# Retention and two feed-forward networks on one core: weight words converted through a parametric ReLU, the hidden layer carried in turns

## The chip, the cores and the metric

The kernel runs on one core of a Trainium2 chip. Its engines work side by side, each through its own queue in order: TensorE (PE; its weight loads are PEld), VectorE (DVE), ScalarE (ACT), GpSimd (POOL) and SyncE (SP), which issues nearly all DMAs. The metric is the device time of one execution in microseconds.

## What is computed

Three steps follow each other: a masked, decaying attention without softmax, and two feed-forward networks over all 2304 tokens. The weights come as float64 and are split in the kernel into two fp32r parts each.

```python
scores = q @ k^T / sqrt(64)                       # 4 batches, 8 heads, 576 tokens, 64 wide
x = (scores * where(i >= j, gamma[h] ** (i - j), 0)) @ v
x = x as (2304, 512)
h = x @ w_in                                      # 512 -> 2048
y = (h * cos(h)) @ w_out                          # 2048 -> 512
h = y @ w2_in
g = where(h >= 1, h, where(h <= -1, 0, (h + 1) ** 2 / 4))
out = g @ w2_out
```

## The kernel before

The tokens of the first network are cut in five blocks (`BLOCKS`: 256 and four times 512), its hidden layer in 16 chunks of 128. A slot is one chunk of one block: `mm1` makes h in 12 matmuls (three products of high and low parts, four slices each), `actA`, `actB` and `actC` make h cos h out of it, `mm2`, two slots later, adds its share of the output in 12 more. Blocks 0 and 1 run interleaved while the weights are still being converted, one chunk of `w_in` (wi) and one of `w_out` (wo) for each pair of slots; a converted wi is also stored (wd) for blocks 2 to 4. The attention of a block's tokens runs before the block (blocks 0 and 1) or between the slots of the block ahead of it. The second network follows in 168 steps of a product scheme with seven products for eight (`product`, `after_product`, `piece`, `group`); its weights are converted in the background of blocks 2 to 4 (`spill_wi2`, `spill_wo2`).

The order on each engine is made by a scheduler, which works from the order of the program, the dependencies, the buffers of the pools and its own estimate of durations. So an operation that falls away can change the order elsewhere.

A weight chunk arrives as 128 x 512 words of 64 bit, seen as two 32-bit halves (raw; the low half is word 0, the high half word 1). Chunks of the first network from number 4 on are loaded twice, the second time shifted by a half word into rsh, so that one shift (L150) makes the low mantissa bits. `begin` (L134) reads the high half as an fp32 and scales it by 2^-112 on ScalarE into X. `signed` (L141 to L143) shifts X to an fp32 exponent and mantissa, takes the sign bit from the high half again and merges it into W, and cuts W to its power of two in X. L158, on ScalarE, rounds W to the high part; L159, on VectorE, makes the low part from C and X. The tag raw has two buffers, X, W and C two each; the next load into a raw buffer waits for the last reader of its high half, which for twice-loaded chunks is L142.

The first network's h stands in PSUM (blocks 0 and 1 copy it to SBUF first, L431). `actA` finds the whole turns by adding and subtracting MAGIC = 1.5 * 2^23 on ScalarE (L433, L434) and subtracts them from h on VectorE (L435); `actB` takes Sin and Square (L440, L441); `actC` multiplies by h (L455) and splits the result in gh (L447, ScalarE) and gl (L448, mostly GpSimd). TensorE's mm2 (L400 to L402) needs both. `copy_out` brings a finished block to SBUF with a factor.

Of the kernel before, what the change touches and what calls it, by code (L numbers as in the profile page):

```python
# [13 lines left out]
AF = mybir.ActivationFunctionType  # L14
ALU = mybir.AluOpType
# [20 lines left out]
LEAD = 3  # L36
TWICE = 4
MAGIC = 1.5 * 2.0 ** 23
INV2PI = 0.15915494309189535
TWOPI = 6.2831854820251465  # L40
SQRT2 = 1.4142135623730951
GAMMA = [1.0 - 2.0 ** (-5 - h) for h in range(H)]
# [23 lines left out]
def retention_moe_kernel(ctx: ExitStack, tc: tile.TileContext, qk, kv, win1, wout1, win2, wout2, mask, vtab, ptab, out):  # L66
    nc = tc.nc
    V, A, G, SY, PE = nc.vector, nc.scalar, nc.gpsimd, nc.sync, nc.tensor
# [25 lines left out]
    def behind(later, earlier):  # L94
        tc.add_manual_dep(later.ins, earlier.ins.name, mybir.DependencyInfo(mybir.DependencyClass.NoSync, mybir.DependencyReason.SCHED_ONLY), reason="pace")
# [31 lines left out]
    def begin(L, i, c, after=None, late=False):  # L127
        raw, raw2 = raws.pop((L, i, c))
        hi = raw[:, :, 1].bitcast(F32)
        if late:  # L130
            X, W = [wp.tile([P, DM], F32, tag=f"wo{k}", name="XW"[k - 1]) for k in (1, 2)]
        else:
            X, W = [cv.tile([P, DM], F32, tag=k, name=k) for k in "XW"]
        i0 = A.activation(X, hi, AF.Copy, scale=2.0 ** -112)  # L134
        if after is not None:
            behind(i0, after)
        return raw, raw2, X, W, late

    def signed(hi, X, W, odd):
        Xi, Wi = X.bitcast(I32), W.bitcast(I32)  # L140
        V.tensor_scalar(out=Xi, in0=Xi, scalar1=3, scalar2=odd, op0=ALU.logical_shift_left, op1=ALU.bitwise_or)  # L141
        V.scalar_tensor_tensor(out=Wi, in0=hi, scalar=-0x80000000, in1=Xi, op0=ALU.bitwise_and, op1=ALU.bitwise_or)  # L142
        V.tensor_scalar(out=Xi, in0=Wi, scalar1=-0x800000, scalar2=None, op0=ALU.bitwise_and)  # L143

    def convert(begun, o, after=None):
        raw, raw2, X, W, late = begun
        lo, hi = raw[:, :, 0], raw[:, :, 1]
        C = wp.tile([P, DM], I32, tag="wo3", name="C") if late else cv.tile([P, DM], I32, tag="C", name="C")
        if raw2 is not None:
            i0 = V.tensor_scalar(out=C, in0=raw2.bitcast(I32)[:, 1:1 + 2 * DM:2], scalar1=7, scalar2=None, op0=ALU.logical_shift_left)  # L150
        else:
            i0 = V.tensor_scalar(out=C, in0=hi, scalar1=23, scalar2=None, op0=ALU.logical_shift_left)
        if after is not None:
            behind(i0, after)
        if raw2 is None:
            V.scalar_tensor_tensor(out=C, in0=lo, scalar=9, in1=C, op0=ALU.logical_shift_right, op1=ALU.bitwise_or)
        signed(hi, X, W, 1)
        A.activation(o[:, 0, :], W, AF.Copy)  # L158
        return V.scalar_tensor_tensor(out=o[:, 1, :], in0=C, scalar=2.0 ** -43, in1=X, op0=ALU.mult, op1=ALU.mult)  # L159

# [2 lines left out]
    def make_wi1(c, begun, after=None):  # L163
        t = wr.tile([P, 2, DM], F32R, tag="wi", name="wi")
        convert(begun, t, after)
        SY.dma_start(out=wd[0, 0, c], in_=f(t))
        wi[0, c] = t

    def make_wo1(c, begun, after=None):
        t = wp.tile([P, 2, DM], F32R, tag=f"wo{c}", name=f"wo{c}")  # L170
        convert(begun, t, after)
        wo[0, c] = t

    def spill_wo2(c, begun):
        t = wp.tile([P, 2, DM], F32R, tag="wo5", name="cw") if begun[-1] else wr.tile([P, 2, DM], F32R, tag="wi", name="cw")
        done.append(convert(begun, t))
        SY.dma_start(out=wd[1, 1, c], in_=f(t))
# [4 lines left out]

    def to_fp32(begun, v):
        raw, _, X, W, _ = begun
        signed(raw[:, :, 1], X, W, 0)
        V.scalar_tensor_tensor(out=X, in0=raw[:, :, 0].bitcast(U32), scalar=2.0 ** -52, in1=X, op0=ALU.mult, op1=ALU.mult)
        done.append(V.tensor_tensor(out=v, in0=W, in1=X, op=ALU.add))

# [215 lines left out]
    def copy_out(e, t, y, scale):  # L404
        if e % 2 == 0:
            A.activation(t, y, AF.Copy, scale=scale)
        else:
            V.tensor_scalar(out=t, in0=y, scalar1=scale, scalar2=None, op0=ALU.mult)

    def evac(s):  # L410
        l, c = slots[s]
        if c != NC - 1:
            return
        o, n = BLOCKS[l]
        per = 512 // n
        for e, y in enumerate(yb.pop(l)):
            t = stp.tile([P, 512], F32, tag="st", name="st")
            copy_out(e, t, y, -1.0)
            SY.dma_start(out=yd[:, e * per:(e + 1) * per, o:o + n], in_=t.rearrange("p (k n) -> p k n", k=per))

    mark = [None]

    def actA(s):
        l, c = slots[s]
        n = BLOCKS[l][1]
        h = hp[s][:, :n]
        t = act.tile([P, 512], F32, tag="t", name="t", bufs=3)[:, :n]
        if l < 2:

            hp[s] = xp.tile([P, 512], F32, tag="x", name="hs")  # L430
            A.activation(hp[s][:, :n], h, AF.Copy)  # L431
            h = hp[s][:, :n]
        mark[0] = A.activation(t, h, AF.Copy, scale=INV2PI, bias=MAGIC)  # L433
        A.activation(t, t, AF.Copy, bias=-MAGIC)  # L434
        V.scalar_tensor_tensor(out=t, in0=t, scalar=-TWOPI, in1=h, op0=ALU.mult, op1=ALU.add)  # L435
        rt[s] = t

    def actB(s):
        u = rt[s]
        A.activation(u, u, AF.Sin, scale=0.5)  # L440
        A.activation(u, u, AF.Square, scale=SQRT2)  # L441

    def parts(u, eng):
# [156 lines left out]
    for l in range(2, NBLK):  # L600
        s0, s1 = window[l]
        span = 2 * (s1 - s0) / len(members[l])
        for k, i in enumerate(members[l]):
            g = int(2 * s0 + k * span)
            e = int(2 * s0 + (k + 1) * span) - 1
            e = max(e, g)
# [63 lines left out]
    for k, i in enumerate(first):  # L670
        c = CH[i]
        c.scores()
        c.masked((None, "wo2")[k % 2])
        if k < 2:
            warm(10, c.lastpe)
        if k + 1 < len(first):
            prepped = CH[first[k + 1]].prep()
        c.full()
        c.inner()
        c.state()  # L680
        if k < 2:
            warm(10, c.lastpe)
        lastpost = c.post()
        if k == 2:
            make_wi1(0, begin(0, 0, 0, after=prepped))
        if k == 4:
            make_wo1(0, begin(0, 1, 0, after=prepped))
            load_raw(0, 1, 1)
    make_wi1(1, begin(0, 0, 1))
    for p in range(-9, 0):  # L690
        run_plan(p)
# [57 lines left out]
    for s in range(N1):  # L749
# [3 lines left out]
        if s >= 1:  # L753
            actC(s - 1)
        actA(s)

        after = lastpost if s <= pos_of[1, 0] else None
# [6 lines left out]
        if s >= LAG:  # L764
            mm2(s - LAG)
            evac(s - LAG)
        for x in bgpos.get(s - 2, []):
            spill_2(*x)
        for x in bgpos.get(s, []):
            load_raw(1, *x)  # L770
        actB(s)
        for x in bgpos.get(s - 1, []):
            begun2[x] = begin(1, *x, after=mark[0])
# [27 lines left out]
def _layout(q, k, v, moe_w_in, moe_w_out, moe2_w_in, moe2_w_out):  # L801
    import numpy as np

    qk = np.zeros((NCH, P, 2 * NP * P), q.dtype)
    kv = np.zeros((NCH, P, 2, DM), q.dtype)
    for i, (b, t, n) in enumerate(CHUNKS):
        for j, a in enumerate((q, k)):
            qk[i, :, j * NP * n:(j + 1) * NP * n] = a[b, :, t:t + n, :].reshape(NP, 2, n, D).transpose(1, 3, 0, 2).reshape(P, NP * n)
        for j, a in enumerate((k, v)):
            kv[i, :n, j, :] = a[b, :, t:t + n, :].transpose(1, 0, 2).reshape(n, DM)  # L810

    def bits(w):
        w = np.ascontiguousarray(w)
        return w.view(np.int64)

    def wi(w):
        return bits(w.reshape(KB, P, NC, P).transpose(2, 1, 0, 3).reshape(NC, P, DM))

    def wo(w):
        return bits(w.reshape(NC, P, DM))  # L820

    g = np.array(GAMMA, np.float64)
    i = np.arange(S)
    start = np.array([t for b, t, n in CHUNKS])
    mask = np.triu(np.ones((P, P), np.float32))
    j = np.arange(P)[:, None, None] + start[None, :, None]
    vtab = (g[None, None, :] ** (-j)).astype(np.float32)
    pw = (g[:, None] ** i[None, :] / 8.0).astype(np.float32)
    whole = np.repeat(pw.reshape(NP, 2, 1, S), D, axis=2).reshape(NP, P, S).transpose(1, 0, 2)
    ptab = np.zeros((NCH, P, NP * P), np.float32)  # L830
    for i, (b, t, n) in enumerate(CHUNKS):
        ptab[i, :, :NP * n] = whole[:, :, t:t + n].reshape(P, NP * n)
    return dict(qk=qk, kv=kv, win1=wi(moe_w_in), wout1=wo(moe_w_out), win2=wi(moe2_w_in), wout2=wo(moe2_w_out),
                mask=mask, vtab=vtab, ptab=ptab)
# [27 lines left out]
```

## Time and profile before

| | |
|---|---|
| median of 3 runs | 891.09 us (891.01 to 891.84) |
| span of the profiled execution | 891.1 us; no longer time is given for it |
| TensorE busy | 863.8 us, 97% |
| VectorE busy | 633.9 us, 71% |
| ScalarE busy | 482.2 us, 54% |
| GpSimd busy | 105.5 us, 12% |
| DMA | 210.76 MB, mean 237 GB/s |

The shares are means over stages that differ: VectorE is nearly full in the first 156 us and half empty behind. Rows by stage tell more. In a row of stretches each engine has its busy time and, in brackets, its number of instructions; then the granted clock of TensorE as a share of its full speed, the mean busy share of the 16 DMA engines, and GB/s. In a row of a group stand line, engine, operation, what is written from what, shapes and count; behind the bar busy time, mean ns of one, and the engine's idle time just before these instructions with what ended it.

### The profile page before, as it was taken

Reading aid. Unit: us, or ns where it says so; the run is one execution under the profiler, and the core shown is the slowest. Engines: PE = TensorE matmul, PEld = TensorE weight load, DVE = VectorE, ACT = ScalarE, POOL = GpSimd, SP = SyncE. Lnnn points to the kernel's source line nnn. Section 1 sums busy time; section 2 is a strip of 40 time slices with the busy share of each in tenths; the row PEclk is TensorE's granted clock in tenths of the full one; section 3 lists DMA queues with packets and bytes.
Section 4 is the critical chain, followed back from the end, with each engine's and each line's share of the span. In section 5 each row is a group of like instructions: output and inputs, shape, how many; then the busy total and the mean of one; then the engine's idle time right before and its main releaser. Section 6 shows DMA issues by size and latency. Waiting matters only on the chain.

```text
span 891.1 us, 13579 instructions
## 1 busy us (share of the span) xinstructions
PE 863.8 (97%) x4876; PEld 742.7 (83%) x4876; DVE 633.9 (71%) x1152; ACT 482.2 (54%) x925; POOL 105.5 (12%) x82
## 2 busy tenths in 40 slices
PE   8689998999999999999999999999999999999997
PEld 7677887887888788888888898988889889898896
DVE  3999989765978687978888477685745667555554
ACT  3678878654656675666776634343433435333333
POOL 0013322200112211212222200000000000000000
PEclk9999999999999999999999999999999999999999
DMA  9858989855686978666977787676766765765531
GB/s 335 321 188 308 319 302 313 293 180 180 205 265 206 324 246 312 208 241 217 348 285 242 236 280 263 229 248 194 238 176 198 245 189 191 244 191 181 154 95 72
DMA packets 70435, 210.76 MB, mean 237 GB/s; under 512 B 7648, under 2 KB 12000, under 8 KB 70368
## 3 DMA queue, kind: packets, MB, share of 16 engines
q1 hardware_dynamic: 69792, 208.96, 69.6%
q10 hardware_dynamic: 576, 0.93, 0.3%
q8 instruction: 39, 0.64, 0.3%
q14 instruction: 28, 0.23, 0.1%
HBM read 168.97 MB, written 40.89 MB: 236 GB/s over the span
## 4 chain that ended last, share of the span: by engine, by line
PE 80%; DVE 6%; DMA 4%; ACT 3%; issue 1%; SPq 0%; DVEq 0%; ACTq 0%
PE hq L521 19%; PE h L385 15%; PE bky L400 6%; PE bky L402 5%; PE bky L401 5%; PE bky L573 5%; PE bky L574 5%; PE bky L575 5%; DMA raw<-in_wout_dram 2%; PE bkO L298 1%; PE bkS L574 1%; PE bkO L573 1%; PE bkO L575 1%; PE bkO L385 1%; PE bkS L385 1%
## 5 line engine op out<-in xcount | busy, mean ns | idle before, releaser
L385 PE MATMUL h<-xhl,wi 128*128 128x512 f32 (+1 forms) x864 | 193.5, 371 | 6.5 <-ACT wi L158 4.0
L521 PE MATMUL hq<-xc,wq 128*128 128x384 f32 x1008 | 198.5, 337 | 0.6 <-DVE sC L529 0.3
L521 PEld LDWEIGHTS hq<-xc,wq 128*128 128x128 f32 x1008 | 179.8, 188 | 12.8 <-DVE sC L529 0.6
L385 PEld LDWEIGHTS h<-xhl,wi 128*128 128x128 f32 x864 | 149.7, 189 | 36.2 <-ACT wi L158 5.1
L448 POOL TENSOR_TENSOR gl<-t,gh 128x512 fp32r<-128x512 f32 (+1 forms) x78 | 105.3, 1351 | 400.7 <-ACT gh L447 352.4
L447 ACT ACTIVATE gh<-t 128x384 fp32r<-128x384 f32 (+2 forms) x176 | 96.5, 549 | 57.6 <-DVE t L556 33.6
L555 ACT ACTIVATE t<-t,half 128x384 f32<-128x384 f32 x96 | 58.9, 615 | 107.3 <-DVE t L554 107.3
L400 PE MATMUL bky<-gh,wo 128*128 128x512 f32 x256 | 101.3, 396 | 1.1 <-ACT gh L447 1.1
L401 PE MATMUL bky<-gh,wo 128*128 128x512 f32 x256 | 100.0, 391 | 0.0
L402 PE MATMUL bky<-gl,wo 128*128 128x512 f32 x256 | 88.5, 391 | 0.0
L556 DVE TENSOR_TENSOR t<-t,sC 128x384 f32<-128x384 f32 x96 | 53.2, 556 | 32.9 <-ACT t L555 32.4
L573 PE MATMUL bky<-wo,gh 128*128 128x512 f32 x192 | 75.6, 394 | 0.2 <-ACT gh L447 0.2
L574 PE MATMUL bky<-wo,gh 128*128 128x512 f32 x192 | 75.6, 394 | 0.0
L440 ACT ACTIVATE t<-t 128x512 f32<-128x512 f32 (+1 forms) x80 | 47.0, 587 | 47.9 <-DVE t L435 47.5
L448 DVE TENSOR_TENSOR gl<-t,gh 128x384 fp32r<-128x384 f32 (+1 forms) x98 | 54.1, 555 | 18.1 <-ACT gh L447 17.9
L575 PE MATMUL bky<-wo,gl 128*128 128x512 f32 x192 | 61.0, 394 | 0.0
L554 DVE TENSOR_SCALAR t<-sC 128x384 f32<-128x384 f32 x96 | 34.3, 357 | 36.0 <-ACT sC L541 34.4
L400 PEld LDWEIGHTS bky<-gh,wo 128*128 128x128 f32 x256 | 48.1, 188 | 12.5 <-ACT gh L447 1.8
L402 PEld LDWEIGHTS bky<-gl,wo 128*128 128x128 f32 x256 | 47.6, 188 | 10.2 <-POOL gl L448 0.2
L401 PEld LDWEIGHTS bky<-gh,wo 128*128 128x128 f32 x256 | 48.1, 188 | 9.5 <-issue 0.2
L142 DVE SCALAR_TENSOR_TENSOR W<-raw,X 128x512 int32<-128x512 int32 x64 | 52.3, 818 | 1.2
L141 DVE TENSOR_SCALAR X<-X 128x512 int32<-128x512 int32 x64 | 28.9, 451 | 26.8 <-ACT X L134 26.8
(127 smaller groups left out, 1374.6 us busy)
## 6 DMA issues: line engine op xcount, KB each, us to landing
wq<-wq SPq DMA_DIRECT2D x72, 512.0 KB, 4.1
wi<-wd SPq DMA_DIRECT2D x48, 512.0 KB, 4.9
wo<-wd SPq DMA_DIRECT2D x48, 512.0 KB, 4.2
raw<-in_win_dram SPq DMA_DIRECT2D x32, 512.0 KB, 5.5
raw<-in_wout_dram SPq DMA_DIRECT2D x32, 512.0 KB, 5.3
qkv<-in_qk_dram SPq DMA_DIRECT2D x16, 512.0 KB, 5.6
wd<-wi SPq DMA_DIRECT2D x16, 512.0 KB, 5.0
wq<-tw SPq DMA_DIRECT2D x32, 256.0 KB, 3.1
```

The lines of the kernel that those rows point to most:

```text
L385: PE.matmul(hp[s][:, :n], w[:, a, kb, :], x[b][:, kb, :], start=(i == 0), stop=(i == 3 * KB - 1))
L400: PE.matmul(o, w[:, 0, es], a, start=first and e % per == 0, stop=False, skip_group_check=True)
L401: PE.matmul(o, w[:, 1, es], a, start=False, stop=False, skip_group_check=True)
L402: PE.matmul(o, w[:, 0, es], b, start=False, stop=last, skip_group_check=True)
L447: A.activation(a, u, AF.Copy)
L448: eng.tensor_tensor(out=b, in0=u, in1=f(a), op=ALU.subtract)
L521: lastmm[0] = PE.matmul(o, w[:, a, kb, :], x[b][:, kb, :], start=first and i == 0, stop=i == 5, skip_group_check=True)
L555: A.activation(t, t, AF.Square, scale=0.5, bias=half)
L556: V.tensor_tensor(out=t, in0=t, in1=h, op=ALU.max)
L573: PE.matmul(y, a[:, js], w[:, 0, :], start=n == 0, stop=False)
L574: PE.matmul(y, a[:, js], w[:, 1, :], start=False, stop=False)
L575: PE.matmul(y, b[:, js], w[:, 0, :], start=False, stop=n == NC - 1)
```

## The change

Two edits. The first takes the sign of a weight word along in the scaling. `begin` uses Prelu in place of Copy, with alpha = 2^32: a positive word gets the factor 2^-112, a negative one 2^-112 * 2^32. The extra 32 in the exponent field lands in the sign bit when the word is shifted left by three. `signed` therefore needs neither the high half nor the merging operation L142; its first shift writes W directly. This concerns all 64 conversions.

The second carries h in turns: the table of decay powers of the attention is divided by 2 pi as well, so that x and h come out divided by 2 pi. `actA` adds MAGIC in its one ScalarE operation, and the VectorE operation behind it subtracts MAGIC and h at once. Sin takes the factor pi, and the copy-out of a block the factor -2 pi in place of -1.

```diff
-        i0 = A.activation(X, hi, AF.Copy, scale=2.0 ** -112)
+        i0 = A.activation(X, hi, AF.Prelu, scale=2.0 ** -112, alpha=2.0 ** 32)
...
-    def signed(hi, X, W, odd):
+    def signed(X, W, odd):
         Xi, Wi = X.bitcast(I32), W.bitcast(I32)
-        V.tensor_scalar(out=Xi, in0=Xi, scalar1=3, scalar2=odd, op0=ALU.logical_shift_left, op1=ALU.bitwise_or)
-        V.scalar_tensor_tensor(out=Wi, in0=hi, scalar=-0x80000000, in1=Xi, op0=ALU.bitwise_and, op1=ALU.bitwise_or)
+        V.tensor_scalar(out=Wi, in0=Xi, scalar1=3, scalar2=odd, op0=ALU.logical_shift_left, op1=ALU.bitwise_or)
         V.tensor_scalar(out=Xi, in0=Wi, scalar1=-0x800000, scalar2=None, op0=ALU.bitwise_and)
...
-            copy_out(e, t, y, -1.0)
+            copy_out(e, t, y, -TWOPI)
...
-        mark[0] = A.activation(t, h, AF.Copy, scale=INV2PI, bias=MAGIC)
-        A.activation(t, t, AF.Copy, bias=-MAGIC)
-        V.scalar_tensor_tensor(out=t, in0=t, scalar=-TWOPI, in1=h, op0=ALU.mult, op1=ALU.add)
+        mark[0] = A.activation(t, h, AF.Copy, bias=MAGIC)
+        V.scalar_tensor_tensor(out=t, in0=t, scalar=-MAGIC, in1=h, op0=ALU.add, op1=ALU.subtract)
...
-        A.activation(u, u, AF.Sin, scale=0.5)
+        A.activation(u, u, AF.Sin, scale=TWOPI / 2)
...
-    pw = (g[:, None] ** i[None, :] / 8.0).astype(np.float32)
+    pw = (g[:, None] ** i[None, :] / (8.0 * TWOPI)).astype(np.float32)
```

Lines of the changed kernel stand one to three above: L134 is L133 there, L141 and L142 together L140, L143 is L141, L150 is L148, L159 is L157, L385 is L383, L435 is L432, L455 is L452.

VectorE's queue in the ramp, where the first wi chunk is converted between the steps of the attention (R: masked scores; xs, xhl: the finished tokens; T: the running state). Before:

```order
L141 TENSOR_SCALAR X<-X 128x512
L351 TENSOR_TENSOR xs<-bky_266,pt 128x512
L142 SCALAR_TENSOR_TENSOR W<-raw,X 128x512
L152 TENSOR_SCALAR C<-raw 128x512
L143 TENSOR_SCALAR X<-W 128x512
L156 SCALAR_TENSOR_TENSOR C<-raw,C 128x512
L159 SCALAR_TENSOR_TENSOR wi<-C,X 128x512
L359 TENSOR_TENSOR xhl<-xs,xhl 128x4x128
L309 TENSOR_TENSOR R<-bky_333,msk 128x512
```

The same place now:

```order
L140 TENSOR_SCALAR W<-X 128x512
L349 TENSOR_TENSOR xs<-bky_266,pt 128x512
L141 TENSOR_SCALAR X<-W 128x512
L150 TENSOR_SCALAR C<-raw 128x512
L157 SCALAR_TENSOR_TENSOR wi<-C,X 128x512
L154 SCALAR_TENSOR_TENSOR C<-raw,C 128x512
L307 TENSOR_TENSOR R<-bky_333,msk 128x512
```

The merge is gone, the product that makes wi stands ahead of the next chunk's L154, and the mask of the next tokens' scores ahead of xhl.

TensorE's queue in the ramp, around its first matmuls on weights (h<-xhl,wi); T, qkv and R are the attention's operands. Before:

```order
L385 MATMUL h<-xhl,wi 128x256 x12
L320 MATMUL bky_333<-qkv,T 128x128 x4
L325 MATMUL bky_332<-qkv 64x64 x8
L333 MATMUL bky_333<-R,qkv 64x128 x8
L325 MATMUL bkS<-qkv 64x64 x8
L320 MATMUL bkO<-qkv,T 128x128 x4
```

The same place now:

```order
L318 MATMUL bky_333<-qkv,T 128x128 x4
L323 MATMUL bky_332<-qkv 64x64 x8
L331 MATMUL bky_333<-R,qkv 64x128 x8
L323 MATMUL bkS<-qkv 64x64 x8
L296 MATMUL bky_440<-qkv 64x64
L383 MATMUL h<-xhl,wi 128x256 x3
L318 MATMUL bkO<-qkv,T 128x128 x4
```

A group of the attention now goes ahead of slot 0, of which three matmuls come first and nine later.

VectorE's queue in the middle of the blocks 0 and 1, from the first shift of a wi chunk to the end of the wo chunk behind it. Before:

```order
L141 TENSOR_SCALAR X<-X 128x512
L142 SCALAR_TENSOR_TENSOR W<-raw,X 128x512
L143 TENSOR_SCALAR X<-W 128x512
L455 SCALAR_TENSOR_TENSOR t<-t,hs 128x256
L159 SCALAR_TENSOR_TENSOR wi<-C,X 128x512
L141 TENSOR_SCALAR X<-X 128x512
L150 TENSOR_SCALAR C<-rsh 128x512
L142 SCALAR_TENSOR_TENSOR W<-raw,X 128x512
L435 SCALAR_TENSOR_TENSOR t<-t,hs 128x512
L143 TENSOR_SCALAR X<-W 128x512
L435 SCALAR_TENSOR_TENSOR t<-t,hs 128x256
L159 SCALAR_TENSOR_TENSOR wo_1291<-C,X 128x512
```

The same place now:

```order
L140 TENSOR_SCALAR W<-X 128x512
L141 TENSOR_SCALAR X<-W 128x512
L148 TENSOR_SCALAR C<-rsh 128x512
L157 SCALAR_TENSOR_TENSOR wi<-C,X 128x512
L452 SCALAR_TENSOR_TENSOR t<-t,hs 128x512
L432 SCALAR_TENSOR_TENSOR t<-t,hs 128x256
L140 TENSOR_SCALAR W<-X 128x512
L452 SCALAR_TENSOR_TENSOR t<-t,hs 128x256
L141 TENSOR_SCALAR X<-W 128x512
L148 TENSOR_SCALAR C<-rsh 128x512
L157 SCALAR_TENSOR_TENSOR wo_1261<-C,X 128x512
```

Both merges are gone; around them the operations of the slots (L432, L452) have other neighbours, but the pattern of a pair is the same. On ScalarE the changed program has one load of an activation table, as the kernel before.

## Rows read from the trace of the kernel before

**Rows 1.** Stretches: window, its length, then PE, PEld, DVE, ACT, POOL

```profile
0.00:22.00 22.00, 17.88 (x192) 16.17 (x194) 7.82 (x17) 7.37 (x22) 0.20 (x4) 1.00 0.95 334
22.00:45.00 23.00, 16.09 (x234) 14.05 (x232) 20.84 (x42) 14.78 (x44) 0.93 (x1) 1.00 0.89 324
45.00:67.00 22.00, 18.54 (x118) 15.61 (x113) 20.52 (x43) 16.07 (x33) 4.08 (x2) 0.92 0.55 185
67.00:156.00 89.00, 84.73 (x486) 72.81 (x485) 83.03 (x148) 75.50 (x164) 26.98 (x21) 1.00 0.89 310
156.00:250.00 94.00, 91.11 (x628) 75.07 (x628) 68.28 (x113) 52.93 (x97) 13.91 (x11) 1.00 0.64 220
250.00:868.00 618.00, 617.45 (x3151) 534.00 (x3150) 423.15 (x774) 308.77 (x555) 59.37 (x43) 1.00 0.69 230
```

**Rows 2.** Timeline of TensorE: start us, length us, instruction, two widths

```profile
251.11 0.39 PE L400 MATMUL bky<-gh,wo 128*128 128x512 f32 x1
...
252.47 0.39 PE L400 MATMUL bky<-gh,wo 128*128 128x512 f32 x1
...
68.38 0.28 PE L400 MATMUL bkS<-gh,wo 128*128 128x256 f32 x1
...
68.98 0.28 PE L400 MATMUL bkS<-gh,wo 128*128 128x256 f32 x1
```

**Rows 3.** Groups of TensorE by shape, 67 to 156 us: first and last of eleven

```profile
L385 PE MATMUL h<-xhl,wi 128*128 128x512 f32 x106 | 27.0, 391 | 0.0
...
L401 PE MATMUL bkS<-gh,wo 128*128 128x256 f32 x22 | 6.2, 282 | 0.0
```

**Rows 4.** Waits, 22 to 67 us: in total, times, longest

```profile
PE h L385 <- ACT wi L158: 4.0, 4, 1.7
```

**Rows 5.** Stretches, L142 alone: window, its length, VectorE busy

```profile
22.00:67.00 45.00, 4.69 (x7) 0.96 0.72 256
67.00:156.00 89.00, 17.53 (x22) 1.00 0.89 310
156.00:250.00 94.00, 5.11 (x6) 1.00 0.64 220
```

**Rows 6.** Stretches, L434 alone: ScalarE busy

```profile
67.00:156.00 89.00, 10.07 (x20) 1.00 0.89 310
```

**Rows 7.** Timeline at 136 us: a raw buffer's last readers and its next load

```profile
136.39 0.67 ACT L134 ACTIVATE X<-raw 128x512 f32<-128x512 f32 x1
...
137.61 0.69 DVE L142 SCALAR_TENSOR_TENSOR W<-raw,X 128x512 int32<-128x512 int32 x1
...
138.37 0.33 SPq L118 DMA_DIRECT2D raw<-in_wout_dram  x1
```

**Rows 8.** Chain that ended last, at 121 us: start, length

```profile
121.40 7.47 DMA raw<-in_wout_dram
```

**Rows 9.** Groups by line and shape, whole span

```profile
L142 DVE SCALAR_TENSOR_TENSOR W<-raw,X 128x512 int32<-128x512 int32 x64 | 52.3, 818 | 1.2
L134 ACT ACTIVATE X<-raw 128x512 f32<-128x512 f32 x64 | 42.0, 660 | 5.5 <-DMA raw<-in_wout_dram 3.1 <-DMA raw<-in_win_dram 2.3 <-DVE wi L159 0.2
L434 ACT ACTIVATE t<-t 128x512 f32<-128x512 f32 x64 | 39.7, 623 | 0.3
L455 DVE SCALAR_TENSOR_TENSOR t<-t,h 128x512 f32<-128x512 f32 x40 | 27.2, 681 | 5.8 <-ACT t L441 5.6
L435 DVE SCALAR_TENSOR_TENSOR t<-t,h 128x512 f32<-128x512 f32 x40 | 27.2, 680 | 8.2 <-ACT t L434 8.2
L555 ACT ACTIVATE t<-t,half 128x384 f32<-128x384 f32 x96 | 58.9, 615 | 107.3 <-DVE t L554 107.3
L447 ACT ACTIVATE gh<-t 128x384 fp32r<-128x384 f32 x96 | 49.9, 520 | 33.9 <-DVE t L556 33.6
```

**Rows 10.** Stretch of one microsecond: the clock stands behind the five engines

```profile
49.00:50.00 1.00, 1.00 (x6) 0.90 (x6) 1.00 (x3) 1.00 (x2) 0.93 (x1) 0.50 0.39 141
```

**Rows 11.** Timeline of ScalarE at the start

```profile
1.17 1.28 ACT L634 ACT_TABLE_LOAD   x1 [1.17 <-PEq L845]
```

More of the change, by code (lines that the diff above doesn't have):

```diff
@@ L38 @@
 MAGIC = 1.5 * 2.0 ** 23
-INV2PI = 0.15915494309189535
 TWOPI = 6.2831854820251465
@@ L156, in convert @@
             V.scalar_tensor_tensor(out=C, in0=lo, scalar=9, in1=C, op0=ALU.logical_shift_right, op1=ALU.bitwise_or)
-        signed(hi, X, W, 1)
+        signed(X, W, 1)
         A.activation(o[:, 0, :], W, AF.Copy)
@@ L184, in to_fp32 @@
         raw, _, X, W, _ = begun
-        signed(raw[:, :, 1], X, W, 0)
+        signed(X, W, 0)
         V.scalar_tensor_tensor(out=X, in0=raw[:, :, 0].bitcast(U32), scalar=2.0 ** -52, in1=X, op0=ALU.mult, op1=ALU.mult)
```

## The prediction

> **What bounds the kernel now.** I read the stretches of the span first, then the waits of the engine that the stretches point to. From 250 us to 868 us TensorE is busy all the time (617.45 of 618 us) [rows 1]: there hardly anything that VectorE or ScalarE saves can show, and this is 69% of the span. In the first 22 us the DMA engines are 95% busy at 334 GB/s while the first inputs arrive [rows 1], and there is no work yet that the change touches. What can move is the stretch from 22 to 250 us. I call 22 to 67 us the ramp (attention of the first tokens), 67 to 156 us the feed stage (blocks 0 and 1, each weight chunk converted just before its use), and 156 to 250 us the hand-over (attention of block 2, then its first slots). TensorE's idle time is 6.91 + 3.46 = 10.4 us in the ramp, 4.3 us in the feed stage and 2.9 us in the hand-over [rows 1]. VectorE is the full engine there: 20.84 + 20.52 of 45 us in the ramp, 83.03 of 89 in the feed stage [rows 1]. ScalarE has 75.50 of 89.
>
> Idle time understates the loss, since a matmul's shown length overlaps the next one. The 512-column matmuls at 251.11 and 252.47 us are six apart, so 0.227 us each, though each is drawn 0.39 us long; five of 256 columns take 0.60 us, 0.12 each [rows 2]. The feed stage holds 486 matmuls [rows 1]: 218 with 512 columns and 268 with 256 [rows 3], which is 218 x 0.227 + 268 x 0.12 = 81.7 us. Of its 89 us, 7.3 are therefore the most that any relief can give back.
>
> In the ramp the largest single reason is the weight conversion: TensorE waits 4.0 us, in four pieces, for L158, the ScalarE copy that follows L142 [rows 4].
>
> **What the change removes.** First, L142, one VectorE operation for each of 64 conversions, mean 818 ns [rows 9], 52.3 us in all: 7 with 4.69 us in the ramp, 22 with 17.53 us in the feed stage, 6 with 5.11 us in the hand-over [rows 5]. The other shifts keep their count and shape; the first now writes W and not X. In order on VectorE nothing is put in L142's place, and in the feed stage a pair of twice-loaded conversions is eight rows of shifts and products where it was ten. VectorE there falls from 83.0 to 65.5 us of 89.
>
> Second, L434, a ScalarE operation for each slot of the first network: 39.7 us in its 64 wide ones [rows 9], 10.07 us of all in the feed stage [rows 6], where ScalarE falls from 75.5 to 65.4. Its subtraction moves into the VectorE operation L435, which keeps one instruction. Its new pair of operations (add, subtract) is not in the trace, but L455 (add, multiply) and L435 (multiply, add), the same shapes from the same memories, take 681 and 680 ns [rows 9], so I take no change. The scale factors in the Sin, in the table of decay powers and in the block's copy-out ride on operations that are there.
>
> Third, a buffer is freed sooner. For most chunks the word's high half was last read by L142, and the next load into that buffer is issued when L142 ends: in one case L134 starts at 136.39, L142 ends at 137.61 + 0.69 = 138.30, and the load goes out at 138.37 [rows 7]. Now L134 alone reads it (for the chunks loaded twice), and the load can go at 136.39 + 0.67 + 0.07 = 137.13, 1.2 us sooner. The chain that ended last runs through such a load, 7.47 us from 121.40 [rows 8], so a round of the buffer, 7.47 + 1.98 = 9.45 us, was longer than TensorE's work on a chunk pair (24 x 0.227 + 24 x 0.12 = 8.3 us). It becomes about 8.2.
>
> **What it adds.** L134's Copy turns into a Prelu with an alpha. No Prelu is in the trace. The nearest rows: L134 itself takes 660 ns and a Copy-like L434 of the same size 623, while an ACTIVATE with one operand more (L555, with the tile half) takes 615 ns against 520 of L447 at the same 384 columns [rows 9]. So Prelu costs between 37 ns less and 95 ns more, at most 22 x 0.095 = 2.1 us of the feed stage's ScalarE, which has just lost 10. I take nothing, the value of the row it replaces, and keep 2.1 us for the range; the cover is ScalarE's 23.6 us of free time there. The Trainium skill ("ScalarE activation tables: per-element evaluation and per-set limits", section What a function is on this engine) says that with the same operands an instruction costs the same whichever table it reads; by that the term is nothing too, and no run shows it yet.
>
> Could Prelu evict the table that Sin needs? One table load takes 1.28 us [rows 11]. If each conversion needed one to Prelu and one back, the feed stage's ScalarE would have 65.4 + 22 x 2.56 = 121.7 us for 89, and the program would end some 33 us later there and some 18 us later in the ramp, near 940 us. The order of the changed kernel has a single table load on ScalarE, as before, so I give this less than 1 in 100. The Trainium skill ("ScalarE: Activation LUTs", section Table sets: the hidden batching unit) has the rule behind it: alternating functions of different sets pays a load at each switch.
>
> **What moves.** The scheduler has written a new order. In the ramp TensorE's first matmuls on weights stood ahead of a group of attention matmuls and now stand behind it, split in 3 and 9. Slot 0's result is due later, but in the old trace TensorE also stalls there on attention, so the attention chain going first is as likely a gain. The spills, the reloads and the queue of SyncE keep their counts, and GpSimd's queue its order.
>
> **The sum**, from the execution shown: its span is 891.1 us, as is the median of the runs (891.09), so nothing is added around it.
> Ramp: 4 us. Seven L142 give 4.7 us on an engine that is 92% busy and ahead of TensorE; bounds 1 (the new order eats most) and 8 (most of the idle 10.4).
> Feed stage: 6 us. Bounds 0 and 7.3. The DMA engines moved 310 GB/s there, at 0.89 of their time; at the 334 of the first stretch [rows 1] the same bytes need 89 x 310/334 = 82.6 us, so their limit is 6.4.
> Hand-over: 2 of its idle 2.9, with 5.1 us of VectorE gone and L434 out of the chain that frees each slot; bounds 0 and 3.
> 250 us to 430 us: 1, from stalls too short to show as idle; bounds 0 and 2. Behind that nothing.
> Together 13: 891.1 - 13 = **878 us**.
>
> TensorE's clock adds a little doubt: at 49 to 50 us it stood at 0.50, the 1.2 GHz level, after the gaps of the ramp [rows 10], and the stretch to 67 us has 0.92 on the mean [rows 1], worth 0.08 x 22 = 1.8 us. A denser ramp may keep it; a second such fall would cost as much again.
>
> **The rivals.**
> The DMA engines are next in line: at 0.89 of their time in the feed stage they may not go faster, loads issued 1.2 us sooner just land later, and the stage keeps its 89 us but for 1. For it: the load of 7.47 us on the chain. Against: 334 GB/s is shown. Then 4 + 1 + 1 + 1 = 7 us, **884 us**.
> All of it frees: ramp 8, feed stage 7.3, hand-over 3, then 2, in all 20, **871 us**. For it: VectorE at 93% with a fifth of its load gone.
> Slower: waits for loads move to the head of ScalarE's queue. L134 waits there for its load, and gh (L447) and hs, which TensorE needs, stand behind it. Before, VectorE was late and hid this. If each of the 24 twice-loaded chunks makes TensorE wait x longer, the time is 891.1 - 8 (gains outside, with ramp at 4) + 24x: slower from x = 0.41 us. If half of the 1.2 us that a load starts sooner came back as wait, x = 0.6, **897 us**. Against: before L134 ScalarE was idle only 5.5 us in all 64 [rows 9].
> It is no gain in practice: the new order takes back in the ramp what L142 gives, and Prelu costs its 95 ns: about **891 us**.
>
> **How the numbers follow.** Forecast (874 to 882) 0.51, DMA next (882 to 888) 0.21, all frees (868 to 874) 0.14, below 868 0.02, no gain 0.06, slower 0.06. The range 868 to 888 holds 0.86. A difference of 0.2% (1.8 us) is about what a measurement of this kernel can tell from none: faster 0.88, same 0.06, slower 0.06.
>
> **What would show it.** Right: VectorE at about 66 of 80-odd us in the feed stage, no more than 660 ns for Prelu, the raw load issued right behind Prelu, TensorE's waits for L158 and gh fewer, and all stages behind 430 us as long as they were. Wrong: the same waits in the feed stage with a DMA as releaser, Prelu above 750 ns, a longer ramp, or a stretch behind 430 us that changed length.

## The result, and the profile of the changed kernel

| | before | changed |
|---|---|---|
| median, runs side by side | 891.05 us (889.95 to 891.84, 4 runs) | 879.96 us (878.45 to 882.57, 4 runs) |
| ratio | | 0.9878, 95% interval 0.9856 to 0.9900 |
| span of the profiled execution | 891.1 us | 876.7 us |
| VectorE busy | 633.9 us, 71% | 591.5 us, 67% |
| ScalarE busy | 482.2 us, 54% | 444.6 us, 51% |

The change is 1.2% faster, and the forecast of 878.0 us is 2 us off. The two spans differ by 14.4 us, the medians by 11.1. In every run that has both, the time is 1.8 us above the span (878.45 against 876.7 in the changed kernel's profiled execution). So the profiled execution of before took some 892.9 us, a little more than the runs shown of it.

The same stretches as in [rows 1], read from the changed kernel (window, length, PE, PEld, DVE, ACT, POOL, granted clock, DMA share, GB/s):

```profile
22.00:45.00 23.00, 18.70 (x251) 16.96 (x252) 20.96 (x44) 15.61 (x45) 0.73 (x1) 0.85 0.92 334
45.00:67.00 22.00, 21.29 (x125) 18.53 (x125) 21.36 (x44) 17.60 (x36) 6.31 (x4) 1.00 0.77 276
67.00:156.00 89.00, 89.00 (x522) 78.96 (x522) 71.72 (x137) 73.75 (x158) 26.03 (x23) 1.00 0.97 347
156.00:250.00 94.00, 93.04 (x664) 75.89 (x663) 63.05 (x103) 43.48 (x76) 13.55 (x10) 1.00 0.59 202
```

From 67 to 156 us TensorE has no visible idle time left (89.00 of 89, it was 84.73), with 522 matmuls in place of 486. The waits of before there were these (in total, times, longest); the same view of the changed kernel is empty.

```profile
PE bkS L400 <- ACT gh L447: 2.8, 3, 1.4
PE bky L400 <- ACT gh L447: 0.8, 1, 0.8
PE bkS L402 <- POOL gl L448: 0.6, 2, 0.3
```

The groups by line and shape that answer to [rows 9], and a raw buffer's release, which answers to [rows 7]:

```profile
L133 ACT ACTIVATE X<-raw 128x512 f32<-128x512 f32 x64 | 42.1, 661 | 0.0
L432 DVE SCALAR_TENSOR_TENSOR t<-t,h 128x512 f32<-128x512 f32 x40 | 27.3, 682 | 30.2 <-ACT t L431 30.2
```

```profile
122.03 0.66 ACT L133 ACTIVATE X<-raw 128x512 f32<-128x512 f32 x1
122.71 0.33 SPq L117 DMA_DIRECT2D raw<-in_win_dram  x1
```

Prelu costs 661 ns where Copy cost 660, and never waits (idle 0.0). The load goes out 0.02 us after it ends.

Where the time went is best read at events that both programs have, the start of certain matmuls in the timelines (us):

| start of | before | changed | gain so far |
|---|---|---|---|
| first mm2 of block 0 | 46.78 | 44.62 | 2.2 |
| first mm2 of block 1 | 62.44 | 57.17 | 5.3 |
| mm2 of block 0, chunk 12 | 151.09 | 138.60 | 12.5 |
| mm2 of block 0, chunk 15 | 176.05 | 159.11 | 16.9 |
| first mm2 of block 2 | 224.42 | 207.88 | 16.5 |
| first mm2 of block 4 | 430.99 | 412.93 | 18.1 |
| last mm2 of block 4 | 511.68 | 495.63 | 16.0 |
| product 24 | 557.83 | 541.80 | 16.0 |
| product 48 | 610.27 | 595.98 | 14.3 |
| end of the span | 891.1 | 876.7 | 14.4 |

### The profile page after: what moved, and what is told of

Its sections match the earlier page's. It is cut to its first block, busy times and chain, and to the rows that moved or that the text cites. A ratio compares the mean times of both kernels' runs of the same rounds, so it can differ in the third digit from the quotient of the medians.

```text
span 876.7 us, 13305 instructions
## 1 busy us (share of the span) xinstructions
PE 857.4 (98%) x4876; PEld 740.6 (84%) x4876; DVE 591.5 (67%) x1088; ACT 444.6 (51%) x845; POOL 103.5 (12%) x82
## 4 chain that ended last, share of the span: by engine, by line
PE 89%; DVE 5%; DMA 4%; ACT 1%; issue 1%; SPq 0%; ACTq 0%; DVEq 0%
PE h L383 19%; PE hq L518 18%; PE bky L398 7%; PE bky L400 7%; PE bky L399 7%; PE bky L570 5%; PE bky L571 5%; PE bky L572 5%; PE bkO L331 1%; PE bkS L383 1%; PE bkO L383 1%; PE bkO L296 1%; PE bkO L572 1%; PE bkO L570 1%; PE bkS L571 1%; PE bkS L572 1%
## 5 line engine op out<-in xcount | busy, mean ns | idle before, releaser
L383 PE MATMUL h<-xhl,wi 128*128 128x512 f32 (+1 forms) x864 | 193.0, 369 | 0.2 <-DVE wi L157 0.2
L383 PEld LDWEIGHTS h<-xhl,wi 128*128 128x128 f32 x864 | 150.0, 188 | 28.7 <-DVE wi L157 0.4
L445 POOL TENSOR_TENSOR gl<-t,gh 128x512 fp32r<-128x512 f32 (+1 forms) x78 | 103.3, 1326 | 385.9 <-ACT gh L444 328.2
L400 PE MATMUL bky<-gl,wo 128*128 128x512 f32 x256 | 91.9, 391 | 0.0
L437 ACT ACTIVATE t<-t 128x512 f32<-128x512 f32 (+1 forms) x80 | 46.8, 586 | 40.8 <-DVE t L432 40.5
L445 DVE TENSOR_TENSOR gl<-t,gh 128x384 fp32r<-128x384 f32 (+1 forms) x98 | 54.4, 556 | 16.9 <-ACT gh L444 16.7
L432 DVE SCALAR_TENSOR_TENSOR t<-t,h 128x512 f32<-128x512 f32 x40 | 27.3, 682 | 30.2 <-ACT t L431 30.2
L438 ACT ACTIVATE t<-t 128x512 f32<-128x512 f32 (+1 forms) x80 | 46.5, 583 | 1.4
```

The costliest lines, as they stand in the source:

```text
L383: PE.matmul(hp[s][:, :n], w[:, a, kb, :], x[b][:, kb, :], start=(i == 0), stop=(i == 3 * KB - 1))
L400: PE.matmul(o, w[:, 0, es], b, start=False, stop=last, skip_group_check=True)
L445: eng.tensor_tensor(out=b, in0=u, in1=f(a), op=ALU.subtract)
```

## The experiments

Theory A: the gain is VectorE's time, which L142 no longer takes. Rivals: B, ScalarE's time (L434); C, the sooner release of the raw buffers. Every ratio is against runs of before taken beside the run. Their medians were 892.2 to 892.3 us, a little above the 891.05 us of the table, so runs of different experiments are best compared by their ratios.

**One part alone.** The Prelu without the turns:

```diff
 # the kernel before, and:
+        i0 = A.activation(X, hi, AF.Prelu, scale=2.0 ** -112, alpha=2.0 ** 32)
+    def signed(X, W, odd):      # as in the change, without L142
```

> The changed kernel with the hidden layer back in its old units, so L434 is back on ScalarE; the Prelu stays. Theory A (VectorE's time for the merge was what held TensorE in the ramp and the feed stage): most of the gain stays, about 882 us (9 of the 11 us between the medians). Rival B (ScalarE's operation was what held it): about 888 us.

886.05 us, ratio 0.9929 (0.9913 to 0.9945), some 6 us faster: more than half of the gain, but less than A had expected. In its trace ScalarE is the next full engine: it is busy 79.94 us from 67 to 156 us (73.75 in the changed kernel), and up to 250 us TensorE waits for its gh, which the changed kernel does not:

```profile
PE bky L399 <- ACT gh L446: 4.2, 3, 2.5
```

The turns without the Prelu (all other lines of the change):

```diff
 # the kernel before, and:
+        mark[0] = A.activation(t, h, AF.Copy, bias=MAGIC)
+        V.scalar_tensor_tensor(out=t, in0=t, scalar=-MAGIC, in1=h, op0=ALU.add, op1=ALU.subtract)
```

> The kernel before with the hidden layer in turns alone; the merge L142 stays on VectorE. Theory A: only 2 to 3 us are gained, about 888 us, VectorE still at 83 of 89 us in the feed stage. Rival B: about 882 us.

896.95 us, ratio 1.0055 (1.0034 to 1.0077): 5 us **slower**, though it only takes an operation away. Neither theory had expected that. So B is out as a gain by itself, and the parts don't add: 6 faster and 5 slower make 11 faster together.

**The change with the merge's time put back.** An operation of L142's kind and size, which reads X alone and so holds no raw buffer:

```diff
-        V.tensor_scalar(out=Wi, in0=Xi, scalar1=3, scalar2=odd, op0=ALU.logical_shift_left, op1=ALU.bitwise_or)
+        V.tensor_scalar(out=Xi, in0=Xi, scalar1=3, scalar2=odd, op0=ALU.logical_shift_left, op1=ALU.bitwise_or)
+        V.scalar_tensor_tensor(out=Wi, in0=Xi, scalar=-0x80000000, in1=Xi, op0=ALU.bitwise_and, op1=ALU.bitwise_or)
```

> The changed kernel with a merge operation of the same kind and size as L142 put back on VectorE, but reading X alone, so the raw buffer is still free behind Prelu. Theory A: the VectorE time is back and with it most of the loss, about 887 us. Rival C (the sooner release of the raw buffer, 1.2 us in each round, made the gain): about 880 us, as the changed kernel.

896.23 us, ratio 1.0044 (1.0029 to 1.0059): 64 operations of 731 ns take the whole gain and 4 us more, where A had expected 887 us. The raw loads still go out right behind L133:

```profile
104.14 0.67 ACT L133 ACTIVATE X<-raw 128x512 f32<-128x512 f32 x1
104.83 0.33 SPq L117 DMA_DIRECT2D raw<-in_wout_dram  x1
```

Turns-only has the merge as well and the late release, and its interval (1.0034 to 1.0077) overlaps with this one. So C gives nothing without VectorE's time. A stands, but not all of the step from 880 to 896 us is VectorE's time alone: a second cost came back with the merge, which the next trace shows.

**The change with a late release.** A one-column read of raw on VectorE:

```diff
+        V.tensor_scalar(out=tiny, in0=hi[:, 0:1], scalar1=0, scalar2=None, op0=ALU.bitwise_or)
```

> The changed kernel with a read of one column of raw's high half on VectorE where the merge stood (about 0.1 us each): the time of the merge stays saved, the raw buffer is held as long as before. Theory A: about 881 us. Rival C: about 887 us, with the feed stage near its old 89 us of work.

881.37 us, ratio 0.9887 (0.9867 to 0.9907). This tells little: the scheduler put the read ahead of ScalarE's in part of the rounds, where the load then went out just as soon.

**Why are the turns alone slower?** First guess, D: the clock in the ramp. More of the small matmuls on zeros that the program has in its first two token groups (`warm`), in three or five groups, in the changed kernel, in before and in the turns-only one:

```diff
-        if k < 2:
+        if k < 5:     # k < 3 in the first run
             warm(10, c.lastpe)
```

> The changed kernel with 20 more of the idle-time matmuls on zeros (wt) around the third chunk of the attention, where TensorE waited 3.6 and 2.7 us and its clock fell to 0.50 for 6.8 us. Theory D (the new order's longer stalls in the ramp cost clock as well): the fall goes, up to 3.4 us less, about 877 us. Rival E (TensorE's ramp is set by VectorE alone, the fall lies in its waits): 880 us, no change.

> The same around the first five attention chunks, 60 more matmuls on zeros, some 3.4 us of work if all ran at full clock. Theory D: no fall of the clock ahead of 45 us, 876 to 878 us. Rival E: 880 us, or 882 if the extra matmuls stand in the way of the attention's.

> The kernel before with the same 60 extra matmuls: its profile shows one fall of 3.4 us, so at most 1.7 us to win under theory D, about 890 us; 892 under rival E. Its distance to the run with the changed kernel and the same matmuls is the change without the ramp's clock.

> The turns alone (merge on VectorE) with the 60 extra matmuls. Without them it took 897 us, with 20.5 us of its profile at half clock where the kernel before had 3.4: theory D: those falls go for the most part and it comes to 889 us. Rival F (the turns' new order makes VectorE's waits longer, whatever the clock): 895 us or more.

Ratios 0.9906 (0.9891 to 0.9921) with three groups and 0.9890 (0.9873 to 0.9907) with five, beside 0.9878 without; before itself gets slower, 1.0039 (1.0027 to 1.0052); turns-only stands at 1.0027 (1.0010 to 1.0043) beside 1.0055, which overlap. More matmuls of this kind win nothing. That isn't a full test of D, since in the changed kernel and in before they leave the ramp's mean clock no higher (in turns-only it is 0.92 in place of 0.89). The stretch of the ramp in the changed kernel without and with five groups, then in before without and with them:

```profile
22.00:67.00 45.00, 39.98 (x374) 35.49 (x375) 42.33 (x87) 33.21 (x81) 7.04 (x5) 0.92 0.85 306
```

```profile
22.00:67.00 45.00, 38.92 (x392) 33.91 (x393) 37.96 (x80) 29.45 (x74) 7.46 (x4) 0.92 0.81 284
```

```profile
22.00:67.00 45.00, 34.63 (x345) 29.67 (x341) 41.37 (x84) 30.85 (x76) 5.01 (x3) 0.96 0.72 256
```

```profile
22.00:67.00 45.00, 38.74 (x386) 33.83 (x386) 40.90 (x85) 31.36 (x77) 6.75 (x3) 0.89 0.72 252
```

Second guess, from the trace of turns-only at 60 us. It is called E from here on and is not the rival E of the expectations above (VectorE alone sets the ramp). First before: GpSimd's gl, and VectorE beside it.

```profile
61.94 3.10 POOL L448 TENSOR_TENSOR gl<-t,gh 128x512 fp32r<-128x512 f32 x1 [11.89 <-ACT gh L447]
```

```profile
63.46 0.41 DVE L152 TENSOR_SCALAR C<-raw 128x512 int32<-128x512 int32 x1
64.31 1.28 DVE L435 SCALAR_TENSOR_TENSOR t<-t,hs 128x512 f32<-128x512 f32 x1 [0.43 <-ACT t L434]
```

Now turns-only: the same gl (drawn with the next one), VectorE's last operation before its gap, TensorE's wait, and two stretches.

```profile
61.10 9.84 POOL L447 TENSOR_TENSOR gl<-t,gh 128x512 fp32r<-128x512 f32 x2 [11.50 <-ACT gh L446]
```

```profile
68.45 0.69 DVE L159 SCALAR_TENSOR_TENSOR wi<-C,X 128x512 fp32r<-128x512 int32 x1
```

```profile
PE bky L402 <- POOL gl L447: 4.1, 1, 4.1
```

```profile
60.30:69.00 8.70, 5.77 (x28) 4.62 (x28) 8.70 (x20) 6.09 (x13) 7.89 (x1) 1.00 0.88 268
70.00:76.00 6.00, 5.69 (x22) 5.32 (x23) 1.49 (x3) 2.72 (x7) 1.81 (x3) 0.50 0.43 169
```

A lone gl takes 1.29 us. In before, VectorE stands still at 63.87 us, since L435 waits 0.43 us for ScalarE's L434; gl ends at 65.04, 1.2 us behind the start of that gap, and L435 takes 1.28 us in place of 0.68. In turns-only L434 is gone, VectorE has no gap from 60.30 to 69.00 us, and TensorE gets gl only at 70.31, 1.2 us after VectorE's last operation ends. It waits 4.1 us for it, and from 70 to 76 us its clock stands at 0.50, the 1.2 GHz level. So **GpSimd's operation is shut out while VectorE runs back to back**, and in turns-only the wait for L434, in which it got through, is gone. The run with the merge kept has the same picture (8.70 of 8.70, a wait of 4.1 us). The Trainium skill ("SBUF — State Buffer", section SBUF: two separate sides) says that VectorE, in an instruction with two inputs in SBUF or in a two-port mode, and GpSimd share a pair of ports as an exclusive lock that the one who starts first holds for the whole instruction. The trace agrees, and goes further: here GpSimd lost some 8 us to a row of instructions, not one.

The run of before with five groups of extra matmuls shows the same with L434 in place. VectorE has no gap from 62.00 to 70.80 us, two gl take 10.70 us from 61.98, and TensorE waits 4.8 us:

```profile
62.00:70.80 8.80, 5.21 (x26) 4.06 (x24) 8.80 (x20) 5.78 (x12) 8.80 (x1) 1.00 0.88 293
```

```profile
PE bky L402 <- POOL gl L448: 4.8, 1, 4.8
```

That run is level with before at block 1's first mm2, 6.0 us behind at chunk 4 of block 0 and still 4.7 behind at the end of its span. So in that run the time lost around the lock-out isn't made up, and the gap in before belongs to that order on VectorE, not to L434 as such.

**Test of E.** Turns-only with gl of the two slots in question (2 and 3) on VectorE, and the same in the changed kernel as a control:

```diff
-        gh[s], gl[s] = parts(u, V if pos_of[1, NC - 1] - 1 <= s <= pos_of[1, NC - 1] else G)
+        gh[s], gl[s] = parts(u, V if 2 <= s <= 3 or pos_of[1, NC - 1] - 1 <= s <= pos_of[1, NC - 1] else G)
```

> The turns alone, with the low part gl of two early slots (2 and 3) made on VectorE in place of GpSimd. Theory E (lock-out): in the turns-only run GpSimd's gl stands from 61.10 us for 9.84 us, two operations that take 1.29 and 0.74 us elsewhere, while VectorE has no gap (8.70 of 8.70 us busy from 60.30 to 69.00); TensorE waits 4.1 us for it and its clock then stands at half for 6.83 us, about 3.4 us of work. With these two on VectorE (about 0.7 + 0.4 us more there) the wait goes: 896.95 - 4.1 - 3.4 + 1.1 = 890.5 us, between 889 and 893, and no fall of the clock at 70 us. Theory D2 (VectorE is merely full there and mm2 would wait anyway): 895 to 899.

> The changed kernel with the same two gl on VectorE, as the control. There the gl of slot 2 takes 2.29 us and no TensorE wait stands on it. Theory E: nothing to win, 1.1 us more on VectorE: 879.5 to 882. If the edit is simply the better place for gl, whatever VectorE does: 875 to 878.

895.29 us, ratio 1.0029 (1.0013 to 1.0044) beside 1.0055. By the number alone that is the 895 to 899 us of the other theory, and the two intervals overlap, so no gain in time is shown. The trace tells the two theories apart; its execution took 900.38 us, the longest of the twelve. The wait at 70 us is gone, but the next pair of gl takes 5.80 us, TensorE waits for that, and the clock falls there:

```profile
60.30:69.00 8.70, 8.70 (x53) 7.74 (x52) 8.70 (x19) 6.83 (x15) 0.00 (x0) 1.00 0.71 241
```

```profile
75.22 5.80 POOL L447 TENSOR_TENSOR gl<-t,gh 128x256 fp32r<-128x256 f32 x2 [3.81 <-PE h L385]
```

```profile
PE bkS L402 <- POOL gl L447: 2.8, 1, 2.8
```

```profile
80.00:86.00 6.00, 6.00 (x23) 5.42 (x24) 5.49 (x10) 3.86 (x8) 2.09 (x2) 0.50 0.98 370
```

The expected 890.5 us was wrong in that it took the lock-out for one event; it moves to the next GpSimd operation in a full stretch. The control gives 880.09 us, ratio 0.9859 (0.9840 to 0.9879): nothing to win where gl isn't shut out, as E has it.

E doesn't explain why turns-only ends late. It is 4.6 us behind before at chunk 4 of block 0 (92.20 against 87.57), 1.2 us ahead at block 2's last mm2 (324.93 against 326.12), and 4.0 behind at block 3's last (430.26 against 426.23). So at block 2's end all that the lock-out cost was made up, and the loss that stays comes behind it. There, in its waits from 330 to 430 us, TensorE waits for VectorE itself, where before and the changed kernel wait for nothing:

```profile
PE h L385 <- DVE t L454: 2.4, 2, 1.4
PE bkO L320 <- DVE R L309: 1.1, 1, 1.1
```

In that stretch the conversions for the second network run behind the slots; the run with the merge kept has 2.5 us of the same wait. No run took it apart.

**Less DMA, more VectorE.** The changed kernel with each chunk loaded once:

```diff
-TWICE = 4
+TWICE = 16
```

> The changed kernel with no chunk loaded a second time: 24 loads of 512 KB fewer, 24 VectorE operations of about 0.69 us more, 16.6 us, nearly all between 47 and 176 us. Rival 'DMA is next' (the feed stage's DMA share is 0.97 at 347 GB/s in the changed kernel): fewer bytes make it faster, 872 to 878. Theory A (VectorE's time): the merge's time is back in another form, as in the run that kept it: 890 to 898, with the GpSimd lock-out possible again.

889.60 us, ratio 0.9963 (0.9946 to 0.9979), just below what A gave:

```profile
67.00:156.00 89.00, 85.13 (x488) 75.04 (x488) 80.06 (x154) 67.56 (x144) 41.89 (x21) 0.97 0.61 207
```

With 207 GB/s in place of 347 it is slower than the changed kernel by 0.9963 - 0.9878 of 891 us, 7.6 us. Fewer bytes don't make the kernel faster, and 24 VectorE operations more cost most of the gain, in part through E, which shows again: GpSimd's gl by shape from 60 to 160 us, first in the changed kernel, then here, and TensorE's waits here.

```profile
L445 POOL TENSOR_TENSOR gl<-t,gh 128x512 fp32r<-128x512 f32 x12 | 16.7, 1391 | 43.6 <-ACT gh L444 41.1 <-PE bkO L400 2.5
```

```profile
L445 POOL TENSOR_TENSOR gl<-t,gh 128x512 fp32r<-128x512 f32 x11 | 27.2, 2472 | 35.4 <-ACT gh L444 32.0 <-PE bkO L400 2.8 <-POOL gl L445 0.4
```

```profile
PE bky L400 <- POOL gl L445: 3.4, 1, 3.4
PE bkS L400 <- POOL gl L445: 2.9, 2, 1.9
```

The longer gl stand beside less DMA traffic, so it isn't the DMA that holds GpSimd up.

**The changed kernel's own loss in the ramp.** Its first wi chunk converted one token group later:

```diff
-        if k == 2:
+        if k == 3:
             make_wi1(0, begin(0, 0, 0, after=prepped))
```

> The changed kernel with the first wi chunk converted one token group later in the program's order. In the changed kernel's ramp VectorE waits 3.58 us at the head of its queue for ScalarE's L133, with xs behind it, and TensorE stands 3.6 us at 22.83 us and 2.7 us at 26.19 us, with 6.83 us at half clock. If this order is what the changed kernel loses in the ramp, the conversion behind xs gives 2 to 5 us back: 875 to 878. If the ramp is set by VectorE's work as a whole, the wait only moves: 879 to 882.

The two waits of the changed kernel from 22 to 30 us and its clock behind them, then the one wait of this run:

```profile
PE bky L296 <- DVE xs L349: 3.6, 1, 3.6
PE bky L318 <- DVE R L307: 2.7, 1, 2.7
```

```profile
24.00:25.00 1.00, 0.00 (x0) 0.00 (x0) 1.00 (x3) 1.00 (x5) 0.00 (x0) 0.50 1.18 397
```

```profile
PE bky L318 <- DVE R L307: 4.2, 1, 4.2
```

880.46 us, ratio 0.9867 (0.9841 to 0.9892), as the second of the two expectations said: two waits of 6.3 us together become one of 4.2, and the time stays. No version ran faster than the change by more than the noise.

## Why the prediction was right, step by step

**The bound.** Right, and shown: VectorE's time in the first 250 us is what moves the end. Taking L142 away alone gives 6 us, from a kernel in whose feed stage TensorE waited only 0.6 us for gl. Putting its time back costs all of the gain (896.23 us), or most of it in another form (889.60); but in both of these runs TensorE also waits for gl again, so VectorE's time and the lock-out are not parted there.

**The terms of the sum**, by the table of events:

| term | forecast (bounds) | measured |
|---|---|---|
| ramp, to block 1's first mm2 | 4 (1 to 8) | 5.3 |
| feed stage, from there to chunk 12 | 6 (0 to 7.3) | 12.5 - 5.3 = 7.2 |
| hand-over, to block 2's first mm2 | 2 (0 to 3) | 16.5 - 12.5 = 4.0 |
| to block 4's first mm2 | 1 (0 to 2) | 18.1 - 16.5 = 1.6 |
| behind | 0 | 14.4 - 18.1 = -3.7 |
| sum | 13 | 14.4 |

That the sum came so near is in part luck: the first four terms together came out 5.1 us above the forecast, and the last took 3.7 of it back. The first three were each somewhat low. In the hand-over term the failing step was the window: I took TensorE's idle 2.9 us from 156 to 250 us, while in before block 0 goes on until 177 us and block 1 until 208, and the chunks still gain there; 4.4 of the term came between chunks 12 and 15. "Behind that nothing" was wrong. Of the 3.7 us, 2.0 were given back in block 4 and 1.7 between products 24 and 48, where TensorE now waits 1.1 us for one of the product scheme's sums and before had no wait. The run with the first wi chunk converted later has neither that wait nor that loss there (13.8 us ahead of before at product 24, 13.7 at product 48), so the 1.7 need not belong to the change. No run tested why.

**VectorE's 65.5 us.** It shows 71.72 from 67 to 156 us, but for 522 matmuls in place of 486: 65.5 x 522/486 = 70.4. The rest is longer shifts: L148 takes 645 ns there where L150 took 545.

**L434 counted as a gain.** The step that failed, though the sum came out. I took its 10 us off ScalarE and gave the waits that it ended no place on VectorE. Alone, that edit costs 5 us. A wait for L434 was where GpSimd got through, which explains the 4.6 us lost by chunk 4; the loss that stays to the end comes after 330 us, with waits for VectorE, and its cause is open. The edit pays only once L142 is gone (ratio 0.9929 with Prelu alone, 0.9878 with both): there TensorE waited for ScalarE, 4.2 us for gh. That this wait is what the edit then saved is read from the traces and was not tested. That GpSimd's queue keeps its order was true and not enough; its durations changed.

**Prelu's price of nothing, and the table.** Right: 661 ns, inside the -37 to +95 ns, one table load.

**The sooner release.** It happens (0.02 us behind L133), but there is no sign that it gave anything: with the release and without VectorE's time (merge kept) the gain is gone.

**The rivals.** DMA next: no. The limit of 334 GB/s that I read from the first stretch was no limit, 347 stand in the feed stage, and the run with less traffic isn't faster. All frees (871): not reached, since the ramp kept waits of 3.6 and 2.7 us and 3.7 us were given back. Slower by waits for loads at the head of ScalarE's queue: L133 waits 0.0 us. No gain: the ramp got shorter, not longer.

**The clock.** The ramp's mean fell from 0.96 to 0.92 over 22 to 67 us, 0.04 x 45 = 1.8 us. That is the "second such fall" of the prediction, in another place: 24 us, behind the wait for xs, in place of 49. It cost less than that here, since TensorE stood still anyway for 2.7 of the 6.83 us at half clock.

**Around the span.** I added nothing; it is 1.8 us. Against before's own profiled time the gain is 14.4 us, against the medians 11.1.

## What to carry to other kernels

In a stage where VectorE is full, an operation less on it moves the end, but by less than its own time once the next engine is full: L142 took 17.53 us of the feed stage, and the stage gained 7.2, with TensorE then busy all the time. Before removing a wait of VectorE, look at what GpSimd does in that gap: if TensorE waits for GpSimd's result, the gap may be what lets it through. A new order can close such a gap without any edit to it, as the extra matmuls did. Two edits on engines that feed each other should be timed alone and together, for here one of them is a loss alone and a gain with the other.

## What the runs showed of the hardware

A GpSimd subtraction of 128x512 that takes 1.29 us alone took some 9 us while VectorE ran 8.70 of 8.70 us, and it ended 1.1 us after VectorE's first gap began. Four more traces have the same near 60 us: with the merge kept, with each chunk loaded once, and before and turns-only with five groups of extra matmuls, such a gl took 8.6 to 10.0 us and again ended 1.1 us after the gap's start. The block goes both ways: VectorE's L435 took 1.28 us in place of 0.68 when GpSimd got in first. GpSimd can get in with no gap to be seen: in the changed kernel, from 62.71 us, two gl end after 3.27 us, and the VectorE operations there show who gave way, 0.96 and 1.51 us in place of 0.41.

```profile
63.26 0.68 DVE L157 SCALAR_TENSOR_TENSOR wo<-C,X 128x512 fp32r<-128x512 int32 x1
63.87 0.96 DVE L148 TENSOR_SCALAR C<-rsh 128x512 int32<-128x512 int32 x1
64.75 1.51 DVE L140 TENSOR_SCALAR W<-X 128x512 int32<-128x512 int32 x1
```

What decides who gets in there stays open.
